# Seven weight operands kept in four tiles instead of seven: a fused memory-attention and SwiGLU kernel

## The chip, the cores and the metric

The kernel runs on one core of a Trainium2 chip. The metric is the device time of one execution in microseconds (us). The core has a matrix engine (PE; its weight loads are listed as PEld), VectorE (DVE), ScalarE (ACT), GpSimd (POOL) and SyncE (SP). Each engine works off a queue of its own in order and waits on semaphores for the others. In this kernel all DMA transfers are issued from SP's queue, so a transfer that has to wait holds up every transfer behind it.

## The reference

Input x has 2048 tokens of width 576. Two branches are computed from it and mixed by a gate per token:

```
g = sigmoid(sum(x * gate_w))
a = attention(x) @ wo      # 32 heads of 18, 4 segments of 512 tokens, causal softmax in the segment
                           # mixed per head with a memory M, z that is carried from segment to segment
b = (silu(x @ w_gate) * (x @ w_up)) @ w_down      # hidden width 4608
out = g * a + (1 - g) * b
```

All inputs and outputs are 32-bit floats.

## The kernel before, in words

**Precision.** A 32-bit operand is split into a high part (an ACT copy into the matrix engine's 32-bit format) and a low part (DVE: the operand minus its high part). A product takes three matmuls: high by high, high by low, low by high.

**Stages.** The first stage (to about 222 us) makes q, k, v and the memory. The long stage is the SwiGLU branch, with the softmax attention woven into it. It consists of 72 *units*: two *halves* (two segments of tokens each; half 0 is segments 2 and 3) by 36 hidden tiles of 128 columns. The last stage projects the attention output and mixes.

**A unit.** Gate and up weights of one hidden tile, in their two halves of 256 input rows, are a 2 by 2 block matrix: a11, a12 (gate), a21, a22 (up). The two segments of x in the same two halves of rows are the other one. Their block product is done with seven products in place of eight, so each unit needs seven weight operands: 0 is a11, 3 is a12, 6 is a22; 1 is a21 + a22, 2 is operand 1 minus a11, 4 is a11 minus a21, 5 is a12 minus operand 2. The function `seven(t, j)` (L1025 to L1033) does product j: six matmuls of 128x512 with operand j (L1030: high, high, low for each of two tiles of 128 rows) and one for the remaining 64 input rows (L1033). Each product's result lives in one of three PSUM banks, and the next products accumulate on copies:

- L1093: after product 0, ACT copies its bank into a second bank. Product 2 accumulates on the first bank and has to wait for that copy.
- L1096 (ACT, after product 1), L1100 (DVE, after product 2: writes the bank that product 5 accumulates on), L1103 (ACT, after product 3).
- L1107: after product 4, ACT copies the bank into the one that product 6 accumulates on. Between its release and its need lies only product 5.
- L1110, L1112: the two silus; L1116, L1117: DVE multiplies; the result is split into `hh`, `hl` for the down projection.

**Beats.** After each product, `beat` (called through `tick`) runs what is due, then a share of the down projection (`down_group`, L870, its sums into `ya` on DVE, L880) and a share of the attention generator. A unit has the eight beats 0 to 7 (0 behind product 0, 3 behind product 3, 4 behind product 4, 5 and 6 behind product 5, 7 behind product 6). Every third unit (a *long* one, about 35 us) has 16 down groups in beats 2 to 7; the two between (*short* ones, about 12 us) have none, and no attention in beats 5 to 7 either. What is due in which beat is written down in tables of (beat, ...), and `defer` puts it in the list; numbers of 8 and more fall into the next unit, so 9 is its beat 1.

**Making the operands.** `w_make` prepares the operands of the next unit during the current one. The raw weights g (a11 and a12, 512 columns) and u (a21 and a22) have been loaded a unit earlier. POOL makes the sums of operands 1, 2, 4, 5 into tiles `ws` (L265; beats 1, 2, 5, 7); ACT makes the high part of operand j in beat HIGH[j] (L269, 128x256 each), DVE its low part in beat LOW[j] (L272, 128x256 each). The operand tiles come from one pool of seven buffers, `wop`, so operand j of the next unit takes the buffer of operand j of this one. The operands of the first two hidden tiles are also stored (L275, `wc`) in half 0, and half 1 fetches them back for its first two units (`w_fetch`, L713) in the beats FIRST (first unit) and j + 2 (second unit).

**The turn.** Behind half 0's last unit (unit 35) follow ten more beats without products (beats 8 to 17), in which the rest of the down groups of half 0 is done. `x_second` loads the x of half 1 (L1004, table LOADS), forms its sums on POOL (L1009, SUMS) and splits them on ACT and DVE (PARTS; L137, L138) in unit 34's, unit 35's and the turn's beats; entries with z = 0 use raw tiles, those with z = 1 borrow operand tiles of `wop`. The pieces of x of half 1 are read by the products of unit 36, the first of half 1: product j needs parts (0, j) and (1, j).

## Time and profile before

| what | value |
|---|---|
| three runs | 1716.43, 1718.6, 1718.86 us (median 1718.6) |
| the profiled execution | 1717.93 us |
| its span (first to last instruction) | 1716.2 us |
| PE, DVE, ACT, POOL busy | 99%, 79%, 63%, 55% of the span |
| granted clock of the matrix engine | full in all slices |
| DMA queues' share | 78.8% of 16 engines over the span |

All numbers of the trace are us from the span's start unless a duration in ns is named. A row of a timeline gives the start, the duration, the engine, the line of the kernel, the operation, what is written and read, a count and, in brackets, the idle time of the engine before it and what ended it. A row of the waits gives the waiting instruction, what it waited for, the sum of the waits in us, their number and the longest. Matmuls are pipelined: a 128x512 matmul is listed with about 390 ns, but the next one starts some 215 ns after it, so PE's busy time tells little, and its lost time is read from the idle time and from the waits of PE and PEld.

### The profile page before, as it was taken

Reading aid. Unit: us, or ns where it says so; the run is one execution under the profiler, and the core shown is the slowest. Engines: PE = TensorE matmul, PEld = TensorE weight load, DVE = VectorE, ACT = ScalarE, POOL = GpSimd, SP = SyncE. Lnnn points to the kernel's source line nnn. Section 1 sums busy time; section 2 is a strip of 40 time slices with the busy share of each in tenths; the row PEclk is TensorE's granted clock in tenths of the full one; section 3 lists DMA queues with packets and bytes.
Section 4 is the critical chain, followed back from the end, with each engine's and each line's share of the span. In section 5 each row is a group of like instructions: output and inputs, shape, how many; then the busy total and the mean of one; then the engine's idle time right before and its main releaser. Section 6 shows DMA issues by size and latency. Waiting matters only on the chain.

```text
span 1716.2 us, 34821 instructions
## 1 busy us (share of the span) xinstructions
PE 1703.3 (99%) x11868; PEld 1480.2 (86%) x11868; DVE 1361.4 (79%) x3231; ACT 1085.5 (63%) x2123; POOL 939.7 (55%) x1194
## 2 busy tenths in 40 slices
PE   9999999999999999999999999999999999999999
PEld 7899878888888888888888888888888888888899
DVE  6567588888888889888889777787787788778655
ACT  7666576776676677567666756665666576566411
POOL 4434546666665655656566555565555555555311
PEclk9999999999999999999999999999999999999999
DMA  8653499998998898997979976887778677767634
GB/s 276 232 188 137 165 299 201 228 231 178 220 234 195 181 217 202 182 211 195 201 161 268 282 176 139 178 185 163 148 179 186 144 164 182 161 142 168 191 120 137
DMA packets 524002, 328.05 MB, mean 191 GB/s; under 512 B 411184, under 2 KB 460336, under 8 KB 523824
## 3 DMA queue, kind: packets, MB, share of 16 engines
q1 hardware_dynamic: 523824, 325.83, 78.8%
q8 instruction: 93, 1.52, 0.4%
q14 instruction: 85, 0.70, 0.1%
HBM read 165.76 MB, written 76.09 MB: 141 GB/s over the span
## 4 chain that ended last, share of the span: by engine, by line
PE 85%; DVE 6%; DMA 3%; ACT 2%; issue 2%; POOL 1%; SPq 0%; DVEq 0%; POOLq 0%; ACTq 0%
PE bank L1030 34%; PE bank L870 26%; PE bank L160 10%; PE bank L1033 6%; PE bank L728 4%; PE bank L776 2%; PE bank L777 1%; PE bank L415 1%; DVE hl L975 1%; PE bank L461 1%; DVE scr L734 1%; PE bank L351 1%; DVE dw L975 1%; DMA rh<-rc 1%; DMA draw<-in_wd_dram 0%
## 5 line engine op out<-in xcount | busy, mean ns | idle before, releaser
L761 POOL TENSOR_TENSOR p<-pe,p 128x512 f16<-128x512 f32 x320 | 378.9, 1184 | 408.4 <-DVE p L760 386.8
L870 PE MATMUL bank<-dw,hh 128*128 128x320 f32 (+1 forms) x2304 | 487.1, 304 | 1.8 <-DVE ya L880 1.4
L870 PEld LDWEIGHTS bank<-dw,hh 128*128 128x128 f32 x2304 | 381.0, 189 | 14.4 <-DVE ya L880 3.3
L746 ACT ACTIVATE pe<-bank,mb 128x512 f32<-128x512 f32 (+3 forms) x512 | 248.5, 527 | 193.7 <-DVE mb L734 180.6
L870 PE MATMUL bank<-dw,hl 128*128 128x320 f32 (+1 forms) x1152 | 340.6, 296 | 0.6 <-DVE hl L138 0.6
L734 DVE CUSTOM_DVE_ANT_0 scr<-bank,cm 128x512 bf16<-128x512 f32 (+3 forms) x512 | 245.9, 480 | 6.8 <-PE bank L728 0.2
L880 DVE TENSOR_TENSOR ya<-bank,ya 128x320 f32<-128x320 f32 x352 | 157.9, 453 | 77.3 <-PE bank L870 76.2
L870 PEld LDWEIGHTS bank<-dw,hl 128*128 128x128 f32 x1152 | 217.9, 189 | 1.1 <-DVE hl L138 1.1
L1033 PE MATMUL bank<-xr,rh 128*128 128x512 f32 x504 | 196.3, 390 | 0.0
L754 POOL TENSOR_SCALAR_AFFINE_SELECT pe<-pe 128x256 f32<-128x256 f32 (+1 forms) x320 | 152.2, 476 | 53.3 <-ACT pe L746 48.9
L760 DVE CAST p<-pe 128x512 f16<-128x512 f32 x320 | 159.9, 500 | 0.0
L265 POOL TENSOR_TENSOR ws<-raw 128x256 f32<-128x256 f32 x140 | 116.6, 833 | 18.0 <-DMA raw<-in_wf_dram 5.2
L728 PE MATMUL bank<-kst,qst 108*128 108x512 bf16 (+3 forms) x512 | 124.6, 305 | 0.0
L975 DVE TENSOR_TENSOR hl<-row,hh 128x512 fp32r<-128x512 f32 x119 | 107.6, 905 | 9.3 <-ACT hh L974 8.9
L1033 PEld LDWEIGHTS bank<-xr,rh 128*128 128x128 f32 x504 | 94.6, 188 | 20.4
L1108 DVE TENSOR_TENSOR row<-bank,row 128x512 f32<-128x512 f32 x72 | 49.7, 690 | 61.9 <-ACT bank L1107 61.7
L746 ACT ACT_TABLE_LOAD x69 | 88.5, 1283 | 11.8 <-DVE mb L734 10.8
L1093 ACT ACTIVATE bank<-bank 128x512 f32<-128x512 f32 x72 | 41.9, 582 | 79.6 <-PE bank L1033 76.5
L1110 ACT ACT_TABLE_LOAD x71 | 91.1, 1283 | 1.2
L1103 ACT ACTIVATE row<-bank 128x512 f32<-128x512 f32 x72 | 43.3, 601 | 69.8 <-PE bank L1033 69.6
L265 POOL TENSOR_TENSOR ws<-raw,ws 128x256 f32<-128x256 f32 x70 | 59.4, 849 | 49.8 <-DVE wo__22504 L272 9.7
L160 PE MATMUL bank<-xo,qhi 128*128 128x512 f32 x264 | 83.2, 396 | 1.0 <-ACT vps L400 1.0
(2170 smaller groups left out, 4081.1 us busy)
## 6 DMA issues: line engine op xcount, KB each, us to landing
raw<-in_wf_dram SPq DMA_DIRECT2D x140, 256.0 KB
rh<-rc SPq DMA_DIRECT2D x72, 336.0 KB
dc<-dw SPq DMA_DIRECT2D x36, 576.0 KB
dw<-dc SPq DMA_DIRECT2D x36, 576.0 KB
stk<-q SPq DMA_DIRECT2D x32, 384.0 KB
draw<-in_wd_dram SPq DMA_DIRECT2D x36, 288.0 KB
rc<-rt SPq DMA_DIRECT2D x42, 224.0 KB
vd<-vps SPq DMA_DIRECT2D x8, 912.0 KB
```

Of the source, the lines that this page charges most:

```text
L160: nc.tensor.matmul(t, st[n], mv[n], start=(n == 0), stop=(n == 13))
L265: (nc.gpsimd.tensor_sub if sub else nc.gpsimd.tensor_add)(src[j], p(), q())
L728: nc.tensor.matmul(t[:, c:c + w], qs[:KR, pr, P * i:P * i + P], ks[:KR, pr, 0:w], start=True, stop=True)
L734: nc.vector.tensor_tensor_reduce(scr[:, :w], t[:, c:c + w], cm[:, L - w:L], -SCALE, 3.0e38, OP.add, OP.min, m[:, k:k + 1])
L746: nc.scalar.activation(pe[:, c:c + w], t[:, c:c + w], AF.Exp, bias=m[:, k:k + 1], scale=SCALE)
L754: nc.gpsimd.affine_select(d, d, pattern=pat, compare_op=OP.is_ge, fill=0.0, base=0, channel_multiplier=1)
L760: nc.vector.tensor_copy(p[:, 0], pe)
L761: nc.gpsimd.tensor_sub(p[:, 1], pe, p[:, 0])
L870: nc.tensor.matmul(ts[m], p, q[:, cs], start=(n == 0), stop=(n == 3 * CH - 1))
L880: nc.vector.tensor_add(ya[:, i, cs], t, ya[:, i, cs])
L1030: nc.tensor.matmul(t, w[:, p, z], x[z][:, q], start=first and n == 0, stop=False, skip_group_check=True)
L1033: nc.tensor.matmul(t, rem[:, RPOS[j]], XR[j], start=False, stop=True, skip_group_check=True)
```

## The change

The seven operands are kept in four tiles: a holds operands 0 and 3, b 1 and 2, c 4 and 6, d operand 5. Tiles a, b, c have 512 columns in each of the two parts, d 256, and each has one buffer of its own.

- Sums: operands 1 and 2 are formed side by side in one `ws` tile with one buffer; operand 4 is formed in place over a21 in the raw tile u, so that u holds operands 4 and 6 side by side; operand 5 has a tile `wt`. The sum of operand 5 is formed in beat 4 instead of 7; the other sums stay.
- High and low parts are made per tile: three ACT copies and three DVE subtractions of 128x512 and one each of 128x256 per unit, instead of seven of 128x256. The copies are in beats 4 (a), 3 (b), 7 (c), 6 (d); the subtractions in beats 5, 6, 9, 8.
- The stores of the first two hidden tiles' operands and the fetches in half 1 are per tile (512 KB each for a, b, c). A store follows one beat behind the subtraction. Fetches for half 1's first unit: beats 9, 10 of the turn (a, b), 16, 17 (c, d). For its second unit: beats 4, 3, 8, 6 (a, b, c, d).
- In `x_second` the z = 1 pieces borrow `ws`, d and c. The two that borrow c are loaded in beat 8, the first of the turn, instead of beats 4 and 6 of unit 35; the first is loaded in beat 2 instead of 3. Part (0, 1) moves from beat 4 of unit 35 to beat 17, and the order of the parts in beats 13 to 18 changes.

```diff
-HIGH = (2, 3, 3, 7, 7, 8, 9)
-LOW = (5, 6, 7, 8, 9, 10, 11)
+PAIRS = ((0, 3), (1, 2), (4, 6), (5,))
+HIGH = (4, 3, 7, 6)
+LOW = (5, 6, 9, 8)
...
-LOADS = ((-3, 0, 0), (-2, 0, 1), (3, 1, 0), (4, 1, 3), (4, 0, 3), (5, 0, 2), (5, 1, 1), (6, 1, 2))
+LOADS = ((-3, 0, 0), (-2, 0, 1), (2, 1, 0), (4, 0, 3), (5, 0, 2), (6, 1, 1), (8, 1, 3), (8, 1, 2))
...
-PARTS = ((2, 0, 0), (4, 0, 1), (10, 1, 0), (11, 1, 5), (12, 1, 3), (13, 0, 5), (13, 1, 1), (14, 1, 4), (15, 1, 2),
-         (16, 0, 2), (17, 1, 6), (17, 0, 3), (18, 0, 4), (20, 0, 6))
-FIRST = (9, 10, 11, 15, 17, 17, 19)
+PARTS = ((2, 0, 0), (10, 1, 0), (11, 1, 5), (12, 1, 3), (13, 1, 1), (13, 0, 5), (14, 1, 2), (15, 1, 6),
+         (16, 0, 2), (16, 1, 4), (17, 0, 1), (18, 0, 3), (18, 0, 4), (20, 0, 6))
+FIRST = ((9, 10, 16, 17), (4, 3, 8, 6))
...
-    wc = dram.tile([KEPT, 7, P, 4 * P], F32, name="wc")
+    wc = dram.tile([KEPT, P, 28 * P], F32, name="wc")
...
-    def op_tile():
-        return wop.tile([P, 2, 2, P], F32R, name="wo_")
+    def op_tile(g, shape=None, dtype=F32R):
+        n = len(PAIRS[g])
+        return wop.tile(shape or [P, 2, n, 2, P], dtype, name=f"wo{'abcd'[g]}_", bufs=1)
...
         def total(j, p, q, sub=True):
-            src[j] = rp.tile([P, 2, P], F32, name="ws", bufs=3)
-            (nc.gpsimd.tensor_sub if sub else nc.gpsimd.tensor_add)(src[j], p(), q())
+            if j == 1:
+                src[1] = rp.tile([P, 4, P], F32, name="ws", bufs=1)
+                part[1], part[2] = src[1][:, 0:2], src[1][:, 2:4]
+            elif j == 5:
+                part[5] = src[3] = rp.tile([P, 2, P], F32, name="wt", bufs=1)
+            (nc.gpsimd.tensor_sub if sub else nc.gpsimd.tensor_add)(part[j], p(), q())
...
-        def high(j):
-            ops[j] = op_tile()
-            nc.scalar.activation(ops[j][:, 0], src[j], AF.Copy)
+        def high(n):
+            tile_of[n] = op_tile(n)
+            op_views(ops, n, tile_of[n])
+            nc.scalar.activation(halves(n, 0), flat(n), AF.Copy)
 
-        def low(j):
-            nc.vector.tensor_sub(ops[j][:, 1], src[j], f32(ops[j][:, 0]))
+        def low(n):
+            nc.vector.tensor_sub(halves(n, 1), flat(n), f32(halves(n, 0)))
...
                 (LEAD + 2, lambda: total(4, lambda: a11, lambda: a21)),
-                (LEAD + 4, lambda: total(5, lambda: a12, lambda: src[2]))]
-        for j in range(7):
-            todo += [(HIGH[j], lambda j=j: high(j)), (LOW[j], lambda j=j: low(j))]
+                (LEAD + 1, lambda: total(5, lambda: a12, lambda: part[2]))]
+        for n in range(4):
+            todo += [(HIGH[n], lambda n=n: high(n)), (LOW[n], lambda n=n: low(n))]
             if half == 0 and f < KEPT:
-                todo.append((LEAD + j + 3, lambda j=j: keep(j)))
+                todo.append((LOW[n] + 1, lambda n=n: keep(n)))
...
-            return [(j + 2 if f else FIRST[j], lambda j=j: one(j)) for j in range(7)]
+            return [(FIRST[f][n], lambda n=n: one(n)) for n in range(4)]
...
-                r[z, q] = wop.tile([P, L], F32, name="wo_") if z else raw_tile()[:, :L]
+                if not z:
+                    r[z, q] = raw_tile()
+                elif q == 0:
+                    r[z, q] = rp.tile([P, L], F32, name="ws", bufs=1)
+                elif q == 1:
+                    r[z, q] = op_tile(3, [P, L], F32)
+                else:
+                    if not pair:
+                        pair.append(op_tile(2, [P, 2, L], F32))
+                    r[z, q] = pair[0][:, q - 2]
```

More of the change, by code (lines that the diff above doesn't have):

```diff
@@ L644, in gated_mix @@
                 rp = pool(ctx, "rp", 4, side="right")
-                wop = pool(ctx, "wop", 7, side="right")
+                wop = pool(ctx, "wop", 1, side="right")
                 kq = pool(ast, "kq", 1, side="right")
@@ L709, in w_fetch, with one @@
             ops = wops[1, f] = [None] * 7
[L711 to L715 removed]
+            def one(n):
+                t = op_tile(n)
+                op_views(ops, n, t)
+                nc.sync.dma_start(op_flat(t), op_home(f, n))
+            return [(FIRST[f][n], lambda n=n: one(n)) for n in range(4)]
         kp = pool(ast, "kp", 2, side="right")
@@ L997, in x_second @@
         def x_second(new, rest):
-            r = {}
+            r, pair = {}, []
             todo = []
```

28 lines of the change are left out of this document (19 added, 9 removed).

## The prediction

> **What bounds the kernel now.** I read the page's head and its chain first, then the waits of PE and PEld, then the two groups that are rewritten, and last the timelines around single waits.
>
> ```profile
> span 1716.2 us, 34821 instructions
> ...
> PE 1703.3 (99%) x11868; PEld 1480.2 (86%) x11868; DVE 1361.4 (79%) x3231; ACT 1085.5 (63%) x2123; POOL 939.7 (55%) x1194
> ...
> PE 85%; DVE 6%; DMA 3%; ACT 2%; issue 2%; POOL 1%; SPq 0%; DVEq 0%; POOLq 0%; ACTq 0%
> ...
> L1033 PEld LDWEIGHTS bank<-xr,rh 128*128 128x128 f32 x504 | 94.6, 188 | 20.4
> ```
>
> The chain is PE for 85%, and the change takes no matmul away. So it can only give back time in which PE waits for another engine, and it can only cost by new waits of that kind. The waits of PE and of its weight loads say how much there is:
>
> ```profile
> PE bank L1030 <- ACT bank L1107: 2.8, 6, 1.0
> ...
> PEld bank L1030 <- ACT bank L1107: 6.7, 10, 1.4
> PEld bank L870 <- DVE ya L880: 3.3, 6, 0.7
> ...
> PEld bank L1030 <- DVE bank L1100: 1.7, 5, 0.7
> ...
> PEld bank L1030 <- ACT bank L1093: 1.2, 1, 1.2
> ...
> PEld bank L1030 <- DVE wo__10239 L272: 0.3, 1, 0.3
> ```
>
> The idle time of PE (2.8 us for L1107) is too small, as a matmul still drains in it; that of PEld (6.7) is too large, as a weight load normally runs ahead. Taking one load of 188 ns off each wait leaves 6.7 - 10 x 0.188 = 4.8 us for product 6 behind the copy L1107, 1.2 - 0.19 = 1.0 for product 2 behind L1093, and 1.7 - 5 x 0.188 = 0.8 for product 5 behind L1100. That is 6.6 us in all in the products, 0.4% of the span. This is the most that relief of ACT and DVE can bring there; the turn comes on top.
>
> **Part 1: seven copies and seven subtractions per unit become four and four.** The cost of one is read from starts of neighbours that did not wait.
>
> ```profile
> 0.00:1716.00 1716.00, 191.39 (x490) 1.00 0.79 191
> ```
> ```profile
> 0.00:1716.00 1716.00, 281.96 (x490) 1.00 0.79 191
> ```
> ```profile
> 249.34 0.41 ACT L269 ACTIVATE wo__2928<-raw 128x256 fp32r<-128x256 f32 x1
> 249.64 0.41 ACT L269 ACTIVATE wo__2930<-ws 128x256 fp32r<-128x256 f32 x1
> ...
> 924.43 0.65 ACT L137 ACTIVATE xo<-wo__12921 128x512 fp32r<-128x512 f32 x1
> 924.95 0.64 ACT L137 ACTIVATE xo<-wo__12935 128x512 fp32r<-128x512 f32 x1
> ```
> ```profile
> 907.54 0.42 DVE L272 TENSOR_TENSOR wo__12727<-ws,wo__12727 128x256 fp32r<-128x256 f32 x1
> 907.87 0.42 DVE L272 TENSOR_TENSOR wo__12821<-raw,wo__12821 128x256 fp32r<-128x256 f32 x1
> ...
> 914.01 0.69 DVE L975 TENSOR_TENSOR hl<-row,hh 128x512 fp32r<-128x512 f32 x1
> 914.61 0.25 DVE L792 RECIPROCAL rz<-acc 128x16 f32<-128x16 f32 x1
> ```
>
> The first two rows are all the copies (L269) and all the subtractions (L272): 490 each, 70 units by 7 (two units of half 1 fetch theirs). A 128x256 copy holds ACT for 0.30 us (249.34 to 249.64), a 128x512 one for 0.52. Three pairs of 0.60 become three of 0.52: 0.24 us per unit, 17 us of ACT over 70 units. On DVE 0.33 and 0.60 give 3 x 0.06 = 0.18 us per unit, 13 us. Neither engine is the bound, so these sums are worth nothing themselves. What counts is *where* the ACT work sits. Ahead of L1107 (beats 0 to 3) ACT had operands 5, 6, 0, 1, 2, that is 1.50 us; now it has tile b alone, 0.52. So L1107 is reached up to 1.0 us earlier in a unit in which ACT has run without a pause. Behind it (beats 4 to 7) two copies of 0.60 become a, d, c, 1.34 us: the next unit's L1093 comes up to 0.7 us later.
>
> ```profile
> 225.71 0.39 ACT L269 ACTIVATE wo__2628<-ws 128x256 fp32r<-128x256 f32 x1
> 226.01 0.58 ACT L1093 ACTIVATE bank<-bank 128x512 f32<-128x512 f32 x1
> ...
> 233.60 0.42 ACT L269 ACTIVATE wo__2722<-ws 128x256 fp32r<-128x256 f32 x1 [2.03 <-DMA wc<-wo__2473]
> 233.92 0.58 ACT L1107 ACTIVATE bank<-bank 128x512 f32<-128x512 f32 x1
> ...
> 376.11 0.42 ACT L269 ACTIVATE wo__4804<-ws 128x256 fp32r<-128x256 f32 x1 [0.62 <-POOL ws L265]
> ```
> ```profile
> 226.64 0.73 PE L1030 MATMUL bank<-xo,wo__2473 128*128 128x512 f32 x2 [0.77 <-ACT bank L1093]
> ...
> 234.55 0.73 PE L1030 MATMUL bank<-xo,wo__2681 128*128 128x512 f32 x2 [0.96 <-ACT bank L1107]
> ...
> 377.79 0.50 PE L1030 MATMUL bank<-xo,wo__4750 128*128 128x512 f32 x1 [0.41 <-ACT bank L1107]
> ```
>
> *Start (units 0 and 1).* The copy of operand 4 stands right ahead of L1093; in the new order it lies in the first stage. That gives back most of the 0.77. In beat 3, ACT sat 2.03 us in front of L1107, as operand 2's buffer was still being stored. Tile b is finished and stored in the first stage, a beat earlier, so L1107 is free of it: the 0.96 goes. What comes late next is the store of tile c (beat 10), ahead of whose rewriting in beat 7 five beats lie. By PEld's rows the two are 1.0 us and, as the longest of L1107, 1.4 - 0.19 = 1.2 us. I take -2.0 us of these 2.2, between 0 and -2.5.
>
> *Other waits for L1107.* Of the 4.8 us 3.6 are left. The third row of ACT shows the limit: the copy ahead of L1107 waits for POOL's sum, which relief of ACT doesn't remove, and the merged copy can't begin with operand 1 while operand 2's sum is awaited (0.52 behind that wait instead of 0.30). I take two thirds, -2.4, between -3.6 and +1. Of the 0.8 us on L1100 I take -0.3, as ACT's copies come ahead of that addition; between -0.8 and +0.5.
>
> *New lateness.* Tile c's copy in beat 7 waits for product 6, and with a and d it pushes L1093 by up to 0.7 us; the subtraction of a, twice as wide, must end before the third matmul of product 0. The last row of the waits above is such a wait that exists already (0.3 us). I take +0.6 for both, between 0 and +4 (half a dozen places of 0.7).
>
> *POOL and SP.* Operand 5's sum in beat 4 comes ahead of that beat's attention work on POOL and is gone from beat 7: no cost, as its transposes are issued a step later; at most its 0.75 us there. SP has three transfers fewer for each stored or fetched set; nothing waits for that.
>
> **Part 2: the turn.** It is bound by DVE:
>
> ```profile
> 910.00:945.00 35.00, 33.42 (x241) 29.34 (x240) 33.33 (x69) 21.76 (x39) 22.49 (x22) 1.00 1.06 283
> ```
> ```profile
> 915.89 0.63 ACT L137 ACTIVATE xo<-raw 128x512 fp32r<-128x512 f32 x1 [0.53 <-POOL raw L1009]
> ```
> ```profile
> 921.20 0.56 PE L870 MATMUL bank<-dw,hh 128*128 128x320 f32 x2 [0.38 <-ACT hh L137]
> 921.93 0.41 PE L870 MATMUL bank<-dw,hl 128*128 128x320 f32 x1 [0.17 <-DVE hl L138]
> ...
> 944.14 0.84 PE L1030 MATMUL bank<-xo,wo__13063 128*128 128x512 f32 x3
> ```
> ```profile
> 944.17 0.68 DVE L138 TENSOR_TENSOR xo<-raw,xo 128x512 fp32r<-128x512 f32 x1
> ```
>
> The window's columns are PE, PEld, DVE, ACT, POOL: DVE is busy for 33.3 of 35.0 us. Part (0, 1) in beat 4 of unit 35 costs ACT 0.53 of waiting and 0.52 of work on the way to the last unit's silus and `hh`, for which PE then waits 0.38 and 0.17 us. Without it that chain is a good 1.0 us earlier; both waits go, and I take -0.9 for them and the weight loads around them (0 to -2).
>
> In exchange part (0, 1) now takes the place in beat 17 that (0, 3) had: by the last row it ends at 944.85, while product 1, which needs it, started at 944.14. DVE has the same ten parts ahead of it, so what it gains in unit 35 PE gains too: +0.7 us (0 to +1.5). Part (0, 3) in beat 18 has two products of time; nothing.
>
> The two loads of x that now wait for product 6 of unit 35:
>
> ```profile
> 917.97 2.69 SPq L1017 DMA_DIRECT2D xr<-xrd  x3
> ...
> 951.22 0.53 SPq L713 DMA_DIRECT2D wo__13445<-wc  x1
> ...
> 953.24 0.42 SPq L222 DMA_DIRECT2D raw<-in_wf_dram  x1
> ```
> ```profile
> 958.26 0.98 POOL L265 TENSOR_TENSOR ws<-raw 128x256 f32<-128x256 f32 x1 [1.15 <-DMA raw<-in_wf_dram]
> ```
> ```profile
> 953.97 0.62 PE L1030 MATMUL bank<-xo,wo__13414 128*128 128x512 f32 x2
> ```
>
> SP passes beat 8 within the first row, by 920.7. A 256 KB load of these stretches takes 5.0 us from issue to use (953.24 to 958.26), so x is there at 925.7. ACT read it at 924.95 (above): it may wait 0.75 us, and DVE is behind ACT. Nothing for PE; without that cover it would be these 0.75 us.
>
> *Fetch for unit 37.* Beat 4 of unit 36 was passed by SP at 951.22 (operand 2's fetch). There tile a is now fetched, 512 KB, whose high part product 0 needs at 953.97. At the pace of the POOL row, 5.0 us, it lands at 956.2: 2.2 us late. That load also had in front of it what SP issued after 951.22, so 2.2 is the upper bound; the lower is 0; I take +0.9, nearer to the lower for that reason. The Trainium skill, SBUF — State Buffer, The DMA setup-cost knee, puts a transfer at 2 us plus its bytes at 436 GB/s: an estimate of 3.2 us for 512 KB and a wait of 0.5 us, with which the sum would be -3.8 us and the time 1714.8; the trace's row has 5.0 us for half the bytes.
>
> **The sum.** -2.0 - 2.4 - 0.3 + 0.6 - 0.9 + 0.7 + 0.9 = -3.4 us. The profiled execution took 1717.93 us (span 1716.2), which gives 1714.5; the median of the runs, 1718.6, stands 0.67 above it, so I predict 1715.2 us, 0.2% less. 0.2% (3.4 us) is about what a measurement of this kernel can tell from no change.
>
> **The rivals.**
>
> *The relief is eaten.* The turn costs its upper bounds (2.2 and 1.5 instead of 0.9 and 0.7, +2.1) and the POOL sum holds L1107 as it did (-1.0 instead of -2.4): -3.4 + 2.1 + 1.4 = +0.1, 1718.7. For it: the row of 5.0 us and the [0.62 <-POOL]. Against it: the start's waits have nothing to do with either.
>
> *Slower: tile a's subtraction comes late for product 0.* Place: beats 5 and 6, in every long unit and some short ones, where DVE is behind by a whole attention step.
>
> ```profile
> 934.74 1.41 DVE L138 TENSOR_TENSOR xo<-raw,xo 128x512 fp32r<-128x512 f32 x1
> ```
>
> Product 0's third matmul needs the low part 0.43 us (two matmuls) after the product's start. A 128x512 subtraction takes 0.27 us more than a 128x256 (0.69 against 0.42), and with POOL at work 1.41, which is 0.99 more. If the 24 units of one kind in three pay between the two, 0.45 us, that is +10.8, less the 3.4: 1726. It decides from 0.15 us per such unit on, where it has eaten the gain. For it: the wait on L272 that PE's weight loads show already. Against it: DVE's work in beats 0 to 3, ahead of it, falls from four subtractions to 0.33 + 0.60, 0.39 us less. The Trainium skill, SBUF — State Buffer, SBUF: two separate sides, says that a DVE operation with two SBUF inputs and a GpSimd operation that reads SBUF lock each other out for a whole instruction; by that one wide subtraction meets fewer such locks than two narrow ones, and the row of 1.41 us agrees that the lock costs about one POOL instruction.
>
> *More than expected.* All 6.6 us of the products' waits and 2 of the turn go, nothing comes new: 1710.
>
> **How the numbers follow.** Forecast 0.52, eaten 0.18, slower 0.22, more 0.08. The forecast's own range is 1712 to 1717.5. I give seven tenths of it to more than 0.2%, as the products' terms were cut from 6.6 to 4.7 us and leave more room on the fast side than on the other. Faster by over 0.2%: 0.7 x 0.52 + 0.08 = 0.44, and a little of the rival's lower edge, 0.46. Within: 0.30. Slower: 0.24, with the upper edge of the eaten case. The range leaves out the last tenth on each side: 1709.5 to 1724.
>
> **What would show it.** Right: no wait of L1030 on L1093 in unit 0, the sum of PEld's waits on L1107 at 2 us or less; L269's count 280 and its busy time near 160 us; no wait of L870 on `hh` near 921. Product 1 of unit 36 waits for L138, product 0 of unit 37 for a DMA. Wrong: waits of L1030 on L272 in many long units, or on L1093 in short ones; or a wait for raw weights that grows.

## The result, and the profile after

The changed kernel took 1721.36 us (median of 19 runs, 1718.88 to 1724.90) against 1718.94 us for the kernel before (19 runs, 1716.43 to 1720.72). The ratio is 1.0016, with a 95% interval of 1.0010 to 1.0022: it is slower, by 2.4 us. That is less than the 0.2% up to which the prediction speaks of no change, but the interval leaves out 1, and the forecast was 3.4 us the other way. The profiled execution has a span of 1720.4 us (before: 1716.2).

In the changed kernel's listing `seven` has its six matmuls in L1065 (before L1030) and the seventh in L1068; L1128, L1135, L1142, L1147 are the former L1093, L1100, L1107, L1112; L294 and L297 make the high and low parts (L269, L272), L283 the sums (L265), L138 and L139 split (L137, L138), L896 is the down projection (L870), L739 the fetch (L713), L1151 the first multiplication behind product 6 (L1116). Of the attention generator, L754 are the scores (L728), L760 the row maxima `mb` (L734), L772 the exponentials `pe` (L746), L786 their conversion to 16 bits (L760). L1000 and L1001 split `hh` and the down weights `dw` (L974, L975).

The head of the page after, its chain, and the waits of PE and of PEld (total, count, longest):

```profile
span 1720.4 us, 34414 instructions
...
PE 1704.9 (99%) x11868; PEld 1479.0 (86%) x11868; DVE 1324.1 (77%) x3021; ACT 1069.0 (62%) x1913; POOL 962.7 (56%) x1194
...
PE 83%; DVE 4%; DMA 3%; ACT 3%; issue 2%; POOL 2%; SPq 2%; DVEq 0%; POOLq 0%; ACTq 0%
```
```profile
PE bank L1065 <- DVE bank L1135: 2.6, 5, 1.1
...
PE bank L1065 <- ACT bank L1142: 1.1, 4, 0.4
PE bank L1065 <- DMA woa__13034<-wc: 1.0, 1, 1.0
...
PE bank L1065 <- ACT bank L1128: 0.9, 1, 0.9
...
PEld bank L1065 <- DVE bank L1135: 5.7, 9, 1.5
PEld bank L1065 <- ACT bank L1142: 4.3, 7, 0.8
```

And the copies (L294) and the subtractions (L297) over the whole span:

```profile
0.00:1720.00 1720.00, 157.10 (x280) 1.00 0.79 191
```
```profile
0.00:1720.00 1720.00, 229.15 (x280) 1.00 0.79 191
```

The work went down: ACT is busy for 16.5 us less than before, as said, with 280 copies for 490, and DVE for 37 us less, more than the 13 us worked out from starts. The time went up nevertheless. PEld's waits for ACT's copy ahead of product 6 fell from 6.7 to 4.3 us, those for DVE's addition (L1135, before L1100) rose from 1.7 to 5.7, and a DMA is now in the list of PE's waits. The second profiles below take most of the rise for the addition back.

**Unit by unit.** A unit's length is the time from the first matmul of its product 0 to the first one of the next unit's; the last column runs to the kernel's last matmul. This table gives, in us, how much longer the units are than in the profile of before. It is worked out from PE's rows of each trace, and the runs below go by it, since single units repeat far better than whole runs.

| profile | 0, 1 | 2 | 3 to 34 | (of them 4) | 35 | 36 | 37 | 38 to 71 |
|---|---|---|---|---|---|---|---|---|
| before, a second profile | 0.0 | 0.0 | +1.9 | (+1.0) | 0.0 | 0.0 | 0.0 | +1.3 |
| changed | -1.3 | +0.4 | +4.9 | (+1.4) | -1.2 | +2.9 | +0.1 | -0.6 |
| changed, a second profile | -1.2 | +0.4 | +2.7 | (0) | -1.2 | +3.7 | +0.1 | -0.6 |
| fetch of a in beat 3 | -1.3 | +0.4 | +2.7 | (0) | -1.2 | +1.7 | +1.3 | -0.6 |
| fetch in beat 3, other order of parts | -1.3 | +0.4 | +2.8 | (0) | -1.2 | +1.2 | 0.0 | -0.6 |
| part (0, 1) back in beat 4 | -1.3 | +0.4 | +2.7 | (0) | -0.4 | +3.8 | +1.6 | -0.5 |
| part (0, 1) in beat 6, fetch in beat 3 | -1.3 | +0.4 | +3.9 | (+0.9) | +0.4 | 0.0 | +0.8 | -0.6 |
| the same, low parts apart | +0.9 | +1.4 | +0.7 | (0) | +0.4 | 0.0 | +1.2 | -0.3 |
| the same, copies apart too | +0.7 | +1.4 | 0.0 | (0) | +0.4 | 0.0 | +1.0 | -0.1 |
| changed, apart from the third tile on | -1.3 | +0.5 | +1.7 | (+0.6) | -0.8 | +1.8 | +0.1 | +0.4 |
| mixed version | -1.2 | +0.3 | +0.3 | (0) | -0.1 | 0.0 | 0.0 | 0.0 |

The front of the turn (unit 35) gained what was forecast, the start (units 0 and 1) about two thirds of it. The gain was lost in units 2 to 34 and in unit 36. In the middle the same units are longer in both profiles of the changed kernel and in neither of the kernel before: unit 2 by 0.4, 3 by 0.5, 8 by 0.5, 10 by 0.3, 21 by 0.7 and 1.0, 33 by 0.3.

### The profile page after: what moved, and what is told of

It is laid out like the page before. It is cut to its first block, busy times and chain, and to the rows that moved or that the text cites. A ratio compares the mean times of both kernels' runs of the same rounds, so it can differ in the third digit from the quotient of the medians.

```text
span 1720.4 us, 34414 instructions
## 1 busy us (share of the span) xinstructions
PE 1704.9 (99%) x11868; PEld 1479.0 (86%) x11868; DVE 1324.1 (77%) x3021; ACT 1069.0 (62%) x1913; POOL 962.7 (56%) x1194
## 4 chain that ended last, share of the span: by engine, by line
PE 83%; DVE 4%; DMA 3%; ACT 3%; issue 2%; POOL 2%; SPq 2%; DVEq 0%; POOLq 0%; ACTq 0%
PE bank L1065 32%; PE bank L896 25%; PE bank L161 10%; PE bank L1068 5%; PE bank L754 4%; PE bank L802 2%; PE bank L803 1%; DMA kst<-stk 1%; PE bank L440 1%; DVE xo L139 1%; POOL ws L283 1%; PE bank L486 1%; PE bank L376 1%; DVE p L786 1%; POOL p L787 1%
## 5 line engine op out<-in xcount | busy, mean ns | idle before, releaser
L787 POOL TENSOR_TENSOR p<-pe,p 128x512 f16<-128x512 f32 x320 | 385.1, 1203 | 422.2 <-DVE p L786 353.4
L896 PE MATMUL bank<-dw,hh 128*128 128x320 f32 (+1 forms) x2304 | 486.7, 304 | 1.0 <-DVE ya L906 1.0
L896 PEld LDWEIGHTS bank<-dw,hh 128*128 128x128 f32 x2304 | 381.2, 189 | 13.3 <-DVE ya L906 2.6
L896 PE MATMUL bank<-dw,hl 128*128 128x320 f32 (+1 forms) x1152 | 340.4, 295 | 0.0
L772 ACT ACTIVATE pe<-bank,mb 128x512 f32<-128x512 f32 (+3 forms) x512 | 247.7, 525 | 143.8 <-DVE mb L760 132.9
L760 DVE CUSTOM_DVE_ANT_0 scr<-bank,cm 128x512 bf16<-128x512 f32 (+3 forms) x512 | 246.1, 481 | 8.1 <-PE bank L754 1.0
L896 PEld LDWEIGHTS bank<-dw,hl 128*128 128x128 f32 x1152 | 217.9, 189 | 0.0
L780 POOL TENSOR_SCALAR_AFFINE_SELECT pe<-pe 128x256 f32<-128x256 f32 (+1 forms) x320 | 164.8, 516 | 58.6 <-ACT pe L772 42.1
L1068 PE MATMUL bank<-xr,rh 128*128 128x512 f32 x504 | 196.4, 390 | 0.0
L786 DVE CAST p<-pe 128x512 f16<-128x512 f32 x320 | 175.0, 547 | 0.0
L754 PE MATMUL bank<-kst,qst 108*128 108x512 bf16 (+3 forms) x512 | 124.6, 305 | 0.8 <-ACT pe L772 0.7
L1068 PEld LDWEIGHTS bank<-xr,rh 128*128 128x128 f32 x504 | 94.6, 188 | 20.4
L1001 DVE TENSOR_TENSOR hl<-row,hh 128x512 fp32r<-128x512 f32 x119 | 96.6, 812 | 2.7 <-ACT hh L1000 2.2
L1142 ACT ACTIVATE bank<-bank 128x512 f32<-128x512 f32 x72 | 42.1, 584 | 70.5 <-PE bank L1068 70.2
L1128 ACT ACTIVATE bank<-bank 128x512 f32<-128x512 f32 x72 | 41.9, 582 | 66.6 <-PE bank L1068 62.5
L400 POOL TENSOR_TENSOR q<-qr,q 128x512 bf16<-128x512 f32 x36 | 44.6, 1238 | 67.8 <-ACT q L399 60.7
```

The lines of the kernel that those rows point to most:

```text
L754: nc.tensor.matmul(t[:, c:c + w], qs[:KR, pr, P * i:P * i + P], ks[:KR, pr, 0:w], start=True, stop=True)
L760: nc.vector.tensor_tensor_reduce(scr[:, :w], t[:, c:c + w], cm[:, L - w:L], -SCALE, 3.0e38, OP.add, OP.min, m[:, k:k + 1])
L772: nc.scalar.activation(pe[:, c:c + w], t[:, c:c + w], AF.Exp, bias=m[:, k:k + 1], scale=SCALE)
L780: nc.gpsimd.affine_select(d, d, pattern=pat, compare_op=OP.is_ge, fill=0.0, base=0, channel_multiplier=1)
L786: nc.vector.tensor_copy(p[:, 0], pe)
L787: nc.gpsimd.tensor_sub(p[:, 1], pe, p[:, 0])
```

## The experiments

### Is one execution enough? Second profiles of both kernels

Both kernels ran once more, unchanged.

> The kernel before once more, unchanged, for a second profile of it: it tells which differences between the lengths of units are the change's and which belong to one execution. Theory: the units' lengths agree within 0.1 us except where transfers end a wait (units 4, 21, 37), where up to 1 us may come or go. If units 2, 3, 8 or 10 differ by 0.3 us or more between the two profiles of the same kernel, the sums over units show nothing.

> The changed kernel once more, unchanged, for a second profile of it. Theory: units 2, 3, 8, 10 and 33 are longer than before by the same 0.3 to 0.5 us again, units 0, 1 and 35 shorter by the same 0.65, 0.65 and 1.2; unit 4's 1.35 and unit 37's wait for its fetch come or go.

Measured: 1720.73 and 1721.32 us, one run each; the lengths are in the table. Units 2, 3, 8, 10 and 33 repeat within 0.1 us in each kernel. Unit 4 does not, in either: in the second profile of the kernel *before* it is 1.0 us longer and unit 5 0.7; units 12, 65 and 71 differ too, by 0.4 to 0.7, which the expectation did not have. The waits of the two second profiles, first before, then changed:

```profile
PEld bank L1030 <- ACT bank L1107: 7.0, 10, 1.4
PEld bank L1030 <- DVE bank L1100: 3.5, 7, 1.1
```
```profile
PEld bank L1065 <- ACT bank L1142: 4.6, 8, 0.8
...
PEld bank L1065 <- DVE bank L1135: 4.2, 7, 1.2
```

Between these two the waits for the addition differ by 0.7 us, not by 4.0: unit 4 waits for it for 1.5 us in the first profile of the changed kernel and for 1.1 in the second of before. Of what is left in the changed kernel, 1.2 us lie in unit 36, at the turn.

The rows of DVE and PE in unit 4, first the changed kernel, then DVE's in the second profile of before:

```profile
298.30 0.62 DVE L264 TENSOR_TENSOR rt<-rr,rt 128x448 fp32r<-128x448 f32 x1 [2.44 <-DMA rc<-rt]
...
299.79 1.27 DVE L297 TENSOR_TENSOR woc__3483<-raw,woc__3483 128x512 fp32r<-128x512 f32 x1
...
301.68 0.68 DVE L1135 TENSOR_TENSOR bank<-bank,row 128x512 f32<-128x512 f32 x1
...
302.42 1.65 PE L1065 MATMUL bank<-xo,woc__3483 128*128 128x512 f32 x6 [1.06 <-DVE bank L1135]
```
```profile
298.99 0.63 DVE L252 TENSOR_TENSOR rt<-rr,rt 128x448 fp32r<-128x448 f32 x1 [2.31 <-ACT pe L746]
...
302.10 0.69 DVE L1100 TENSOR_TENSOR bank<-bank,row 128x512 f32<-128x512 f32 x1
```

DVE's subtraction for a block of remaining rows (`rt`) waits over 2 us, and the addition behind it comes late. In the changed kernel the row names a store of that block as what it waited for; the row of before names an exponential. So unit 4 is no effect of the change, and 1.4 of the 4.9 us in the first profile's middle belong to that execution.

### Is it the place of tile c's low part on DVE?

The waits for the addition suggested that the wide low part of c, in beat 1, stands in front of it in DVE's queue. Three runs moved DVE work behind the addition.

```diff
-LOW = (5, 6, 9, 8)
+LOW = (5, 6, 10, 8)
```

> Changed kernel with one number different: the low part of tile c (operands 4 and 6, 512 columns) is made in beat 2, behind the addition that product 5 waits for, and not in beat 1, ahead of it. Theory A (the early units lose because the wide low part of c stands ahead of that addition in VectorE's queue): units 2 to 11 give back 1.5 to 3 us, the weight loads' wait for the addition falls from 5.7 us to below 2.5, time 1718.4 to 1719.9 against the changed kernel's 1721.4. Rival B (the early units lose by the waits for the attention's row block from DRAM, the pairing is neutral): no change, 1721.4. Rival C (all of the loss is in the turn): no change. A new wait can come: product 4 on the low part of c, if VectorE is late; it would be listed as a wait for that tile.

Measured: 1724.38 us, ratio to before 1.0038 (1.0024 to 1.0052): 3 us *slower* than the changed kernel. Expected were 1.5 to 3 us less. PEld's waits for L1135 did fall, to 2.9 us (changed kernel: 5.7 and 4.2); those for L1142 rose to 7.1 (4.3 and 4.6). DVE's, ACT's and PE's rows of unit 1 show why:

```profile
241.98 0.90 DVE L297 TENSOR_TENSOR woc__2753<-raw,woc__2753 128x512 fp32r<-128x512 f32 x1
```
```profile
245.63 0.84 ACT L772 ACTIVATE pe<-bank,mb 128x128 f32<-128x128 f32 x2 [0.96 <-DVE mb L760]
246.36 0.60 ACT L1142 ACTIVATE bank<-bank 128x512 f32<-128x512 f32 x1
```
```profile
247.01 1.65 PE L1065 MATMUL bank<-xo,woc__2753 128*128 128x512 f32 x6 [1.06 <-ACT bank L1142]
```

The low part now stands in front of DVE's row maxima (`mb`); ACT's exponentials wait 0.96 us for those, where they waited for nothing in this place of the changed kernel, and the copy L1142, which has nothing to do with either, is behind the exponentials. Product 6 pays.

```diff
-LOW = (5, 6, 9, 8)
+LOW = (5, 6, 9, 10)
```

> Changed kernel with the low part of tile d (256 columns, 0.33 us of VectorE) in beat 2, behind the addition, and not in beat 0, ahead of it. Rival G in its narrow form (each 0.1 us on VectorE ahead of the addition costs 0.1 us of product 4 in units 2, 5, 8, 11): the waits for the addition fall by 0.3 us each, 1 us in all, 1720.4. Theory H, which the later low part of c suggests (work moved behind the addition delays the row maxima, the exponentials and with them the copy L1142, for which product 6 waits): the sum of waits for L1142 grows by as much as those for the addition fall, 1721 to 1722.

Measured: 1723.60 us, ratio 1.0030 (1.0018 to 1.0041). Rival G in its narrow form fell: the waits for L1135 are 4.3 us, no less than the 4.2 of the second profile, in which unit 4 is not late either. Of theory H only one half came, the waits for L1142 rose to 5.5. The time rose by more than H's 0 to 0.6 us; in the profile 1.2 us of that lie in unit 36's wait for its fetch, which also differs between runs of one kernel.

```diff
+        def low_c(i):
+            nc.vector.tensor_sub(tile_of[2][:, 1, i], u[:, 2 * i:2 * i + 2], f32(tile_of[2][:, 0, i]))
...
+                todo += [(9, lambda: low_c(0)), (11, lambda: low_c(1))]
```

> Changed kernel, the low part of tile c alone in two instructions of 256 columns: operand 4 in beat 1 as now, operand 6 in beat 3, behind the addition. This is the order on VectorE that the kernel before had; tiles, copies and transfers stay paired. Theory A: the same gain as from the later low part, 1 to 2.5 us in units 2 to 11, and no wait of product 4 can come. Rival B or C: no change. If the later low part gains and this one doesn't, it is not the width ahead of the addition but any subtraction in beat 1 that costs.

Measured: 1722.02 us, ratio 1.0017 (1.0008 to 1.0026): no change in time. Units 8 and 10 got shorter by 0.25 us each, but unit 2 got 1.9 us longer. ACT waits there for a transfer; I put that down to the store of c, which had to move back with the last low part and holds up SP's queue:

```profile
250.91 0.63 ACT L294 ACTIVATE woc__2899<-raw 128x512 fp32r<-128x512 f32 x1 [1.71 <-DMA raw<-in_wf_dram]
```

Units 3 to 34 came down from +2.7 to +1.8 us in this profile. So the first theory fell in its simple form: moving one low part behind the addition gained nothing in time in any of the three runs, and another wait took over, most of all in unit 1 in the first of them and in unit 2 in the third.

### Is it the wide copy of c on ACT?

```diff
-HIGH = (4, 3, 7, 6)
+HIGH = (4, 3, 8, 6)
```

> Changed kernel with one number different: ScalarE's copy of tile c in beat 0, behind the copy L1128 (L1093 before), and not in beat 7, ahead of it. The run with a later low part has ended theory A in its first form (the place of the wide low part on VectorE); what is left as theory F: the wide copy of c in beat 7 stands on ScalarE ahead of the splits and of the exponentials on which VectorE and then the matrix engine wait. By F: product 2 of unit 0 waits 0.5 us less (1.1 to 0.6), the waits for the addition L1135 in units 5, 8 and 11 fall from 1.25 to below 0.6 us in sum, time 0.8 to 1.5 us less than the changed kernel's 1721.4. Rival G (VectorE's queue as a whole sets these waits, wherever ScalarE's copy stands): 1721 to 1722, and the low part of c then waits for its copy.

Measured: 1721.61 us, ratio 1.0018 (1.0009 to 1.0027), the time that rival G has. Of F's local parts the first came true and was handed on at once; PEld's waits for the addition in units 5, 8 and 11 fell from 1.8 to 1.4 us in sum, less than F has. PE's rows of units 0 and 1:

```profile
225.64 1.67 PE L1065 MATMUL bank<-xo,wob__2468 128*128 128x512 f32 x6 [0.42 <-ACT bank L1128]
...
229.80 0.39 PE L754 MATMUL bank<-kst,qst 108*128 108x512 bf16 x1 [0.65 <-DMA kst<-stk]
...
245.48 1.67 PE L1065 MATMUL bank<-xo,woc__2769 128*128 128x512 f32 x6 [0.21 <-ACT bank L1142]
```

The wait of product 2 fell from 0.9 to 0.42 us. But the attention step behind it then waited 0.65 us for a transfer, and product 6 of unit 1 had a wait again that the changed kernel had lost. Unit 8 gained 0.4 us as well; in the sum nothing is left.

### Is it the merging itself?

The low parts were taken apart again, seven subtractions in the beats and the order of before, into the four tiles (`low_one` makes the part of one operand in its tile); in a second run the copies too, in the beats of before but for operand 0's, which is in beat 4 and not 2. (Both with part (0, 1) in beat 6 and the fetch in beat 3, see below.)

```diff
+HIGH_ONE = (4, 3, 3, 4, 7, 6, 7)
+LOW_ONE = (5, 6, 7, 8, 9, 10, 11)
...
-        for n in range(4):
-            todo += [(HIGH[n], lambda n=n: high(n)), (LOW[n], lambda n=n: low(n))]
+        for j in range(7):
+            n = next(n for n in range(4) if j in PAIRS[n])
+            i = PAIRS[n].index(j)
+            todo += [(HIGH_ONE[j], lambda n=n, i=i: high_one(n, i)), (LOW_ONE[j], lambda n=n, i=i: low_one(n, i))]
```

> The run before this one with all low parts apart again: seven subtractions of 256 columns in the beats and the order of the kernel before, into the same four tiles, copies still by tile. Theory J (the matrix engine's waits in units 2 to 34 come from VectorE's order; the relief on ScalarE has no part in them): units 3 to 34 give back 0.8 to 1.5 us against the changed kernel; units 1 and 2 lose up to 2 by the later stores. Theory K (the units are held by the chain of row maxima, exponentials and copies as a whole, and what one wait gives the next takes): no more than 0.4 either way in units 3 to 34.

The second run has `HIGH_ONE = (4, 3, 3, 7, 7, 8, 9)`.

> The run before this one with the copies apart as well: seven copies of 256 columns, the copies of operands 3 to 6 in the beats of the kernel before (7, 7, 8, 9), operand 0 in beat 4 with tile a. What is left of the change is then the tiles, the sums, the transfers and the turn. If the merging of instructions is what makes units 3 to 34 longer by 3 us than before, they come back to within 0.7 us of the kernel before; if they stay 1.5 us or more longer, it is the sums and tiles.

Measured: 1722.53 us (1.0021, 1.0013 to 1.0030) and 1721.21 us (1.0017, 1.0008 to 1.0026). The times hide two opposite effects. Units 3 to 34 came back: from +3.0 us (the +3.9 of the run they were made from, without its 0.9 in unit 4) to +0.7 with the low parts apart, to 0.0 with the copies apart too. Units 0 to 2 lost about 3 us. There the stores of the first two hidden tiles have to wait for the last narrow low part, and ACT's copy of c waits 0.3 and 0.8 us for such a store; the mixed version below, with these two tiles as changed, is at -0.9 us in the same units. That the stores alone cost the 3 us is not shown.

So the merging makes the middle longer, the low parts by about 2 us of it and the copies by 0.7. Single units say it best: units 3, 8, 10 and 33 are 0.3 to 0.5 us longer in all six profiles of the table with merged instructions, 1.6 us together, and within 0.15 us of before in all four with narrow ones. But the narrow low parts also stand in the beats of before again, those of operands 5 and 6 behind the addition. Width and place were not told apart.

To see whether this holds in time, the merging alone was undone, from the third hidden tile on, with the turn and the first two tiles as changed:

> Changed kernel with one thing undone: from the third hidden tile on, copies and subtractions are made in seven narrow instructions each, in the order of the kernel before, into the same four tiles; the turn stays as changed. If the merging alone makes units 3 to 34 longer (2.7 us by the lengths of the units), those units stand at 0 against the kernel before, the turn still loses its 1.6 to 3 us there, and the time is 1718.6, 2.7 us under the changed kernel's. If the earlier agreement was chance or hangs on the turn, the time stays above 1720.5.

Measured: 1719.63 us, ratio 1.0006 (0.9997 to 1.0015), against 1.0016 for the changed kernel. That is 1.7 us back of the 2.7 expected, with an uncertainty of about 1.9 us by the two intervals: between the two cases put forward, and by the time alone not clear of noise. In the profile units 3 to 34 stand at +1.7 us, of which 0.95 in units 4 and 5, which vary between executions; units 3, 10 and 33 stand at 0.0.

How the merging does it shows in unit 8. First rows of PE and DVE in the changed kernel, from the start of product 0 to that of product 4, then the same of the mixed version below, where all is apart (its L318 and L1157 are L297 and L1135):

```profile
368.24 1.53 PE L1065 MATMUL bank<-xo,woa__4573 128*128 128x512 f32 x6
...
371.19 0.76 DVE L1001 TENSOR_TENSOR dw<-draw,dw 128x576 fp32r<-128x576 f32 x1 [0.34 <-ACT dw L1000]
371.86 1.23 DVE L297 TENSOR_TENSOR woc__4618<-raw,woc__4618 128x512 fp32r<-128x512 f32 x1
373.01 0.68 DVE L1001 TENSOR_TENSOR hl<-row,hh 128x512 fp32r<-128x512 f32 x1
...
374.75 0.69 DVE L1135 TENSOR_TENSOR bank<-bank,row 128x512 f32<-128x512 f32 x1
...
375.50 1.66 PE L1065 MATMUL bank<-xo,woc__4618 128*128 128x512 f32 x6 [0.34 <-DVE bank L1135]
```
```profile
365.64 1.52 PE L1087 MATMUL bank<-xo,woa__4610 128*128 128x512 f32 x6
...
368.64 0.41 DVE L318 TENSOR_TENSOR woc__4655<-raw,woc__4655 128x256 fp32r<-128x256 f32 x1
...
370.94 0.70 DVE L1157 TENSOR_TENSOR bank<-bank,row 128x512 f32<-128x512 f32 x1
371.55 1.22 DVE L318 TENSOR_TENSOR wod__4675<-wt,wod__4675 128x256 fp32r<-128x256 f32 x1
...
372.27 1.52 PE L1087 MATMUL bank<-xo,woc__4655 128*128 128x512 f32 x6
```

The addition starts 6.5 us after product 0 in the changed kernel, 5.3 us after it with narrow instructions (5.6 in the kernel before). Three things make that up: DVE waits 0.34 us for ACT, which has the whole of c ahead of that copy; the low part of c is twice as wide; and as it runs beside a sum on POOL it takes 1.23 us, where the subtraction of the same width behind it takes 0.68. The Trainium skill, SBUF — State Buffer, SBUF: two separate sides, has DVE operations with two SBUF inputs and GpSimd operations that read SBUF lock each other out for a whole instruction; the row of 1.23 us agrees. This third thing is not the width's: the narrow low part of c, 0.41 us, met no POOL instruction, and the narrow one of d behind the addition, which runs beside one, takes 1.22 us.

PE waits here at product 4, where the prediction had product 5: product 4 writes the bank that the addition reads.

### The turn

```diff
-FIRST = ((9, 10, 16, 17), (4, 3, 8, 6))
+FIRST = ((9, 10, 16, 17), (3, 3, 8, 6))
```

> Changed kernel, in which half 1's second unit fetches tile a in beat 3 (ahead of tile b) in place of beat 4. Theory A and rival C: product 0 of unit 37 no longer waits 1.2 us for the transfer; the fetch is issued 3.5 us earlier and lands ahead of the product; time 1.0 to 1.3 us less than the changed kernel, 1720.2. Rival D (the transfers are limited by the full queues and not by when they are issued): the wait stays at 0.7 us or more, time 1720.9 to 1721.4.

Measured: 1719.59 us, ratio 1.0008 (0.9999 to 1.0017). Product 0 of unit 37 no longer waits. In this profile product 4 of unit 37 waits for tile c instead (PE's row, then SP's issue of that fetch):

```profile
964.91 1.40 PE L1065 MATMUL bank<-xo,woc__13079 128*128 128x512 f32 x5 [1.01 <-DMA woc__13079<-wc]
```
```profile
956.17 0.45 SPq L739 DMA_DIRECT2D woc__13079<-wc  x1
```

That is 8.7 us from issue to use. The next run keeps this fetch.

```diff
-         (16, 0, 2), (16, 1, 4), (17, 0, 1), (18, 0, 3), (18, 0, 4), (20, 0, 6))
+         (16, 0, 1), (16, 1, 4), (17, 0, 2), (18, 0, 3), (20, 0, 4), (21, 0, 6))
```

> Changed kernel with the earlier fetch of tile a (beat 3) and another order of the parts of x at the turn's end: part (0, 1) in beat 16 and (0, 2) in 17, part (0, 4) behind the addition of unit 36 (two beats later) and (0, 6) a beat later. Theory A: the waits in unit 36, product 1 for its part (0.55) and product 4 for the addition behind two parts in one beat (0.9), both go, without new ones: 1.2 to 1.5 us less than the run with the earlier fetch alone (1719.6), so 1718.2. Rival: VectorE has the same work, so product 4 waits for part (0, 4) instead (0.3 to 0.8): 1719.

Measured: 1718.39 us, ratio 1.0003 (0.9994 to 1.0012), so the turn alone brings the changed kernel back to the time of before. Product 1 starts without a wait, but product 4 waits for part (0, 4), more than the rival's 0.3 to 0.8:

```profile
950.86 1.43 PE L1065 MATMUL bank<-xo,woc__12910 128*128 128x512 f32 x5 [0.89 <-DVE xo L139]
```

> The run before this one with tile c's copy in beat 0 as well. If the two gains add up (theory F and the turn's order): 1717.2, below the kernel before (1718.8). If VectorE's queue is what counts (rival G): as the run before this one, 1718.2 to 1719.

Measured: 1720.70 us, ratio 1.0010 (1.0001 to 1.0019). The gains did not add up. The median is 2.3 us above the run before it, though the intervals overlap; in the profile 1.2 us of that are the wait for tile c in unit 37.

The part itself was put back, once to beat 4 (the fetch as changed), once to beat 6 (with the fetch in beat 3). Part (0, 3) goes back to beat 17 with it:

```diff
-PARTS = ((2, 0, 0), (10, 1, 0), (11, 1, 5), (12, 1, 3), (13, 1, 1), (13, 0, 5), (14, 1, 2), (15, 1, 6),
-         (16, 0, 2), (16, 1, 4), (17, 0, 1), (18, 0, 3), (18, 0, 4), (20, 0, 6))
+PARTS = ((2, 0, 0), (4, 0, 1), (10, 1, 0), (11, 1, 5), (12, 1, 3), (13, 1, 1), (13, 0, 5), (14, 1, 2), (15, 1, 6),
+         (16, 0, 2), (16, 1, 4), (17, 0, 3), (18, 0, 4), (20, 0, 6))
```

> Changed kernel with one part of x put back: part (0, 1) is split in beat 4 of unit 35 again, and no longer in beat 17. Theory A, by the terms of the prediction: the waits at the turn's front come back (+1.2 us in unit 35), product 1 of unit 36 waits no more for that part (-0.6), and product 5's wait of 0.9 for the addition behind two parts in one beat becomes about 0.3 as VectorE has one subtraction less to do there (-0.6): in sum 0.0, between -0.5 and +0.7. Rival E (the move of the part is what makes the changed kernel slower): 1.0 us or more less than the changed kernel.

> Changed kernel with the earlier fetch of tile a and part (0, 1) in beat 6 of unit 35, behind both silus (the kernel before had it in beat 4, ahead of them; the changed one in beat 17); the parts at the turn's end are then one fewer. Theory A: unit 35 keeps its gain of 1.2 us, as the part stands behind what hh needs on ScalarE, and unit 36 loses its waits for part (0, 1) and for the addition (1.2 us over the run with the other order): 1717.0 to 1717.6, below the kernel before. Rival: VectorE is full from unit 35 on, the part costs in beat 8 what it saves in beat 17: 1718.4.

Measured: 1720.74 us (1.0010, 1.0002 to 1.0019) and 1720.30 us (1.0010, 1.0001 to 1.0019). In beat 4 the part costs unit 35 0.8 us, less than the 1.2 expected; the rest of that profile is a wait of 3.3 us for the late fetch, by itself. In beat 6 it costs 1.6 us, and frees unit 36 of every wait (0.0). The expectation looked at ACT, where the part is behind the silus. But on DVE, whose rows these are, it is ahead of the multiplication behind product 6, and waits there:

```profile
922.44 0.69 DVE L139 TENSOR_TENSOR xo<-raw,xo 128x512 fp32r<-128x512 f32 x1 [1.00 <-ACT xo L138]
923.05 0.68 DVE L1151 TENSOR_TENSOR row<-bank,row 128x512 f32<-128x512 f32 x1
```
```profile
924.45 0.56 PE L896 MATMUL bank<-dw,hh 128*128 128x320 f32 x2 [0.84 <-ACT hh L138]
```

### All that the runs single out

```diff
-FIRST = ((9, 10, 16, 17), (4, 3, 8, 6))
+FIRST = ((9, 10, 16, 17), (3, 3, 7, 6))
...
+        if half == 0 and f < KEPT:
+            for n in range(4):
+                todo += [(HIGH[n], lambda n=n: high(n)), (LOW[n], lambda n=n: low(n)), (LOW[n] + 1, lambda n=n: keep(n))]
+            return sorted(todo, key=lambda t: t[0])
+        for j in range(7):
...
```

> What the runs so far single out, put together: the first two hidden tiles (whose operands are stored) with merged instructions and early stores as in the changed kernel; all others with seven copies and seven subtractions of 256 columns in the order of the kernel before, in the same four tiles; part (0, 1) back in beat 4 of unit 35; half 1's second unit fetches tile a in beat 3 and c in beat 7. By the sum over the units' lengths of the earlier runs against the kernel before: units 0 and 1 -1.3 us, unit 2 +0.4 to 0, units 3 to 34 0, unit 35 -0.4, unit 36 0, unit 37 0 to +0.8: -1.3, between -1.7 and -0.1, so 1717.4 against 1718.8. Theory K (what one wait gives, the next takes, wherever it is) says instead that units 1 to 3 take back the start's 1.3: 1718.5 or more.

Measured: 1717.19 us against 1718.82 us, ratio 0.9993 (0.9984 to 1.0002). The sum over the units gave 1717.4. It is faster than the changed kernel; against the kernel before the interval still holds 1. In the profile, whose span is 1714.5 us, the longest of PE's waits in the products are these:

```profile
PE bank L1087 <- ACT bank L1164: 1.4, 4, 0.4
...
PE bank L1087 <- ACT bank L1150: 0.9, 1, 0.9
```

L1164 is the copy ahead of product 6, L1150 the one after product 0; the addition is not in PE's list any more (PEld's waits for it are 1.4 us), nor is a fetch.

## Why the prediction was wrong

The range (1709.5 to 1724.0) held the time, but only by its width; the direction was wrong, and slower had a chance of 0.24. By places and the units of the two profiles: units 0 to 2 gave -0.9 and -0.8 us (forecast -2.0), the rest of the middle +4.9 and +2.7 (forecast -2.1; the second profile of before differs by +1.9 itself), units 35 to 37 +1.7 and +2.6 (forecast +0.7). The rival that the relief is eaten came closest, and one half of its mechanism, POOL's sum, is what the rows show; it did not have the merging itself as a cost. By the steps:

- **The start, -2.0.** Right in place, too large. The wait of product 6 in unit 0 went, and units 0 and 1 are 1.3 us shorter. But product 2 waits as long as before (0.9 us for L1128), so the 1.0 us booked for it came to nothing: I took the copy of operand 4 for its cause, as it stands right ahead of the copy in ACT's rows. In both kernels ACT waits just before that for DVE (0.60 and 0.58 us) in a chain of the first stage, and c's wide copy is now a part of that chain (with it away, product 2 waits 0.42 us). Unit 2 is 0.4 us longer.
- **Other waits for L1107, -2.4.** This step failed, and it is the largest. I reasoned from the ACT work that falls away ahead of L1107, though I had named the limit myself: the copy ahead of it waits for POOL's sum. PEld's waits for it fell from 6.7 to 4.3 us, but 2.1 of these 2.4 lie in units 0 and 1; outside the start 0.3 us are left. In five of the seven units in which PEld still waits for L1142 (8, 10, 17, 20, 29), ACT isn't busy ahead of it, but idle for 1.1 to 1.4 us until POOL has the sum for tile b. Behind it come the wide copy and exponentials, and then L1142. Unit 20, first the changed kernel, then before:

```profile
617.18 0.63 ACT L294 ACTIVATE wob__8190<-ws 128x512 fp32r<-128x512 f32 x1 [1.33 <-POOL ws L283]
...
618.43 0.60 ACT L1142 ACTIVATE bank<-bank 128x512 f32<-128x512 f32 x1
```
```profile
615.41 0.42 ACT L269 ACTIVATE wo__8432<-ws 128x256 fp32r<-128x256 f32 x1 [0.79 <-POOL ws L265]
...
616.45 0.60 ACT L1107 ACTIVATE bank<-bank 128x512 f32<-128x512 f32 x1
```

  From the copy's start to L1142 it takes 1.25 us now and took 1.04: the merged copy is longer behind the same sum. In unit 11 the exponentials wait 0.45 us for DVE's row maxima instead; in unit 44 ACT waits for nothing there. The limit of 2 us that I had named was missed.
- **The addition L1100, -0.3.** This step failed with its sign. I looked at the sums of DVE's work ahead of it, less in the changed kernel, not at the widest single piece, nor at the copy of c that this piece has to await. PEld's waits for the addition grew in both pairs of profiles, and units 2 and 8, in which it is late, are 0.4 and 0.5 us longer. With units 3, 10 and 33, where a low part of a, the copy L1142, and the copy L1128 with a low part of b come late, they make up 2.0 of the middle's 3.1 us in the second profile; the runs with all apart put units 3, 8, 10 and 33 on the merging.
- **New lateness, +0.6.** Right in kind. Product 0 of unit 3, 0.5 us longer, waits for the wide low part of a, which took 1.26 us:

```profile
259.80 1.19 PE L1065 MATMUL bank<-xo,woa__2997 128*128 128x512 f32 x4 [0.22 <-DVE woa__2997 L297]
```

  This is the mechanism of the slower rival, but it is met in a few units, not in 24. All subtractions together are busy for 53 us less, where the starts gave 13; that agrees with the inference that fewer of them meet a POOL instruction, but it did not help where PE waits.
- **Turn front, -0.9.** Right: -1.2, no wait for `hh` near 921.
- **Part (0, 1), +0.7.** Right: product 1 waits for L139 (0.40 us of idle time; its second matmul starts 0.57 us late).
- **Part (0, 3) in beat 18, nothing.** This step failed: with (0, 4) in the same beat it delays the addition, and product 4 pays 0.9 us. DVE's rows, then PE's of unit 36:

```profile
947.93 1.95 DVE L139 TENSOR_TENSOR xo<-raw,xo 128x512 fp32r<-128x512 f32 x2
949.80 1.51 DVE L786 CAST p<-pe 128x512 f16<-128x512 f32 x1
...
952.03 0.69 DVE L1135 TENSOR_TENSOR bank<-bank,row 128x512 f32<-128x512 f32 x1
```
```profile
946.92 1.43 PE L1065 MATMUL bank<-xo,wob__12657 128*128 128x512 f32 x5 [0.40 <-DVE xo L139]
...
952.78 1.65 PE L1065 MATMUL bank<-xo,woc__12910 128*128 128x512 f32 x6 [0.77 <-DVE bank L1135]
...
958.82 1.61 PE L1065 MATMUL bank<-xo,woa__13034 128*128 128x512 f32 x6 [0.98 <-DMA woa__13034<-wc]
```

- **Fetch of tile a, +0.9.** Right in kind, too small: 1.2 us by the starts (0.98 of idle time, the last row), 1.9 and 3.3 of idle time in two other profiles. It was issued at 953.91 and used 4.9 us later, near the 5.0 us of the load that I had drawn on; in the second profile and in the run with the part in beat 4 it took 5.8. That it did not cost my upper bound of 2.2 us in the first profile comes from the two other waits in unit 36, which put off the product that needs it. The Trainium skill's 2 us and 436 GB/s (SBUF — State Buffer, The DMA setup-cost knee), an estimate of 3.2 us, does not agree with any of the fetches that were waited for (4.9 to 8.7 us).

What stays open: why unit 21 is 0.4 to 1.0 us longer in every version with the four tiles, those with narrow instructions too, and in neither profile of before; when the transfers of units 4 and 37 come late; and whether the merged low parts cost by their width or by their beats. The sums and the shared tiles were not undone by themselves.

## What to carry to other kernels

The work on an engine in front of a wait need not be what sets it: follow the waiting instruction's own chain back across engines (here a copy, exponentials, a merged copy, and behind that a sum on POOL) before a saving on one engine is booked. Merging two instructions saved 0.08 us of ACT and 0.06 of DVE a pair here, by the starts that the prediction shows, but the merged one needs all its inputs and stands in front of the next as a whole; look at the widest piece ahead of each deadline, on each queue, and at the stores behind it. For changes of 0.2%, lengths of single stretches, with a second profile of both kernels, tell apart what whole runs can't.

## What was not expected of the hardware

Two profiles of the kernel before differ by 2.8 us of span, in five units (4, 5, 12, 65, 71, by 0.4 to 1.0 us each), while nearly all the others repeat within 0.1 us (unit 21 differs by 0.2). In unit 4 of the changed kernel the row names a transfer that ended late; for the other units no run shows the cause. A 512 KB fetch that PE waited for took between 4.9 and 8.7 us from issue to use, in the same stretch of the kernel. And a DVE subtraction of 128x256 beside a POOL instruction took as long as one of 128x512 beside another (1.22 and 1.23 us), where 0.41 and 0.68 are their times alone.
